# Segment loop of a recurrent-memory transformer: P V's middle tile for both heads in one matmul, weight slices asked for at their buffer's release, three loads on SyncE's queue

## The chip, the cores and the metric

The kernel runs on one core of a Trainium2 chip. The metric is device microseconds of one execution; lower is better. Engines are named as in the profile: PE (TensorE matmuls), PEld (its weight loads), DVE (VectorE), ACT (ScalarE), POOL (GpSimd), SP (SyncE, which here only issues DMAs).

## The reference

Everything is bfloat16. x is 2048 x 640.

```python
# part a: 64 segments of 32 rows, in order; mem (8 x 640) goes from one to the next
for s in range(64):
    h = concat([mem, x[32*s:32*s+32]])                   # 40 x 640
    q, k, v = h @ Wq, h @ Wk, h @ Wv                     # 32 heads of 192
    p = softmax(where(mask, q @ k.T * 192**-0.5, -1e9))  # per head, 40 x 40; mask: key < 8 or query >= key
    o = (p @ v).reshape(40, 32*192) @ Wo                 # 40 x 640
    mem, a[32*s:32*s+32] = o[:8], o[8:]
# part b: sliding attention with 8 keys at distance 2, 32 heads of 20
b = dilated_attention(x @ wqkv) @ wo
out = g * a + (1 - g) * b                                # g = sigmoid(sum(x * gate_w))
```

Each segment needs the memory of the segment before, so the 64 steps of part a are a chain.

## The kernel before

The work runs in four stages. From 0 to about 181 us part b and the gate are computed and stored. From 181 to 359 us a prepass projects, for all segments at once, 8 rows of each segment that do not depend on the memory (the "z" rows: their q, k and v go to zpk_dram). From 359.0 to 1652.4 us the segment loop runs (part_a). From there to the end, part_z projects the z rows' attention output through Wo.

In the loop a segment has 32 rows left that depend on the memory. Four heads' columns are put side by side on TensorE: its 128 columns hold four blocks of 32 rows, one for each j in 0 to 3, and every matmul is given a tile position 32j. Nearly all weights stay in SBUF. Fourteen slices of 384 KB (the list STREAM) do not fit: each segment loads them again from a scratch tensor in DRAM (wscr) into five buffers (WBUFS, pool wstream, tile wst). get_unit (L565 to L570) asks for a slice where the program first uses it; the load goes out on SP's queue as soon as the last matmul that read its buffer is done.

The order of PE, ACT and DVE is the order in which the program issues (manual_schedule); SP's order is the scheduler's, as early as the waits allow. One segment, by its lines:

- project (L771): q and k projections, six PSUM tiles (u = 0 to 2 for each); ACT copies each out (c_qk, L784); PE transposes them (t_qk, L792) and DVE copies the result (c_t, L803 and L807).
- s_a, s_b (L825, L834): scores of two halves of the heads, h = 0 and 1; e_exp (L843, ACT), e_mask (L847, DVE), e_norm (L857, PE, sums over the keys), e_recip_a (L862 and L863, ACT, reciprocals), e_recip_b (L869 and L870, DVE, the normalized P).
- m_v (L771): v projections u = 0, 1, 2; c_v copies them out (L881, DVE). V of the z rows (Vz) comes from zpk_dram by a load on ACT's queue (load_vz, L756).
- pv_half(h) (L883 to L906): P V. The 384 columns of two heads are three tiles of 128: t = 0 is the first head's, t = 2 the second's, and t = 1, the middle one, is half of either head. So t = 0 and t = 2 are full-tile matmuls (128 columns of V), t = 1 is made with two 64-column matmuls, each with its own head's P. The r < 2 matmuls (L897) use V of the 32 rows, the third (L902) Vz. A half is 48 matmuls. Its output lies in four PSUM banks: pS (two banks of psS) for j = 0 and 2, and two one-bank tiles px of the pool psx (two buffers) for j = 1 and 3. Below, J0 to J3 are the four outputs.
- c_x (L911) copies the 32 rows of each J out of PSUM, c_z (L918) the z rows' 8 columns into zst; both are shared between ACT ("a") and DVE ("d").
- o_group (L940): the out projection, in two PSUM accumulators, "oa" (384 columns of the output) and "ob" (256), twelve groups of four matmuls each. Groups 0 to 5 of a part use the result of pv_half(0), 6 to 11 that of pv_half(1).
- the copies of the accumulators to whi (L1030 and L1038, ACT), load_z for the next segment (L751, ACT's queue, and a POOL copy, L752), sel (L951, L954), which puts the new memory into the next segment's hT, and tail (L1046, L1050), which adds part b's rows (a4, loaded at L1000 on ACT's queue) and is followed by the store to out_dram (L1056, ACT's queue). hT of the next segment is loaded at L686 on ACT's queue. zst is stored to oz_dram at L1023 on ACT's queue.

Around the change the program's order is

```python
m_v(2, (0, 1, 2)); pos = pv_half(0); c_x(0, pos, (0, 1, 3), "add")
e_norm(1); e_recip_a(1); m_v(2, (3, 4)); c_v(2); e_recip_b(1)
c_x(0, pos, (2,), "a"); c_z(0, pos, (1, 3), "aa"); c_z(0, pos, (0, 2), "dd")
o_group("oa", 0 to 5); pos = pv_half(1); c_x(1, pos, range(4), "adda"); c_z(1, pos, range(4), "adad")
oz store; o_group("ob", 0 to 4); o_group("oa", 6 to 11); whi copy; load_z; o_group("ob", 5 to 11)
```

with the scores of the second half, s_a(2), s_a(3), s_b(1) and e_exp(1), ahead of it. At the loop's start five slices are loaded ahead, and w_ob's last weights (last_loads) are loaded during segment 0; in the last segment load_oz fetches the z rows' attention output into weight tiles that are no longer needed, and the first slice of "oa" goes into such a tile as well (L935).

## Time and profile before

| what | value |
|---|---|
| median of 3 runs | 1710.91 us (1705.75 to 1717.67) |
| the profiled execution | 1710.89 us |
| its span in the trace | 1709.1 us, mean PE clock 0.982 |
| segment loop | 359.0 to 1652.4 us |
| 62 steady segments | 382.8 to 1623.9 us |

In the groups of the profile a row reads: line, engine, operation, output<-input by the program's names, size; then busy us, mean ns of one; then idle time of the engine just before, with what released it. A row of the waits reads: engine, line <- what it waited for: us in total, times, longest. A row of the stretches has: start and end, length, then for PE, PEld, DVE, ACT, POOL busy us and (x instructions), then PE's granted clock, the DMA engines' busy share and GB/s. A row of the timeline reads: start, length, engine, line, operation, output<-input, size, how many; in brackets the idle time before it and what ended it. "issue" is time in which an engine waited for nothing that the profile shows. q1 is SP's DMA queue, q10 ACT's, q8 fetches instructions.

### The profile page before, as it was taken

Reading aid. Unit: us, or ns where it says so; the run is one execution under the profiler, and the core shown is the slowest. Engines: PE = TensorE matmul, PEld = TensorE weight load, DVE = VectorE, ACT = ScalarE, POOL = GpSimd, SP = SyncE. Lnnn points to the kernel's source line nnn. Section 1 sums busy time; section 2 is a strip of 40 time slices with the busy share of each in tenths; the row PEclk is TensorE's granted clock in tenths of the full one; section 3 lists DMA queues with packets and bytes.
Section 4 is the critical chain, followed back from the end, with each engine's and each line's share of the span. In section 5 each row is a group of like instructions: output and inputs, shape, how many; then the busy total and the mean of one; then the engine's idle time right before and its main releaser. Section 6 shows DMA issues by size and latency. Waiting matters only on the chain.

```text
span 1709.1 us, 75634 instructions
## 1 busy us (share of the span) xinstructions
PE 1602.0 (94%) x33193; PEld 888.6 (52%) x33209; DVE 697.0 (41%) x2159; ACT 803.7 (47%) x2082; POOL 60.0 (4%) x124
## 2 busy tenths in 40 slices
PE   7887999989999999999999999999999999999989
PEld 4544544445555555555555555555555545555559
DVE  3765333234444443444444443444443334444430
ACT  3877423234455444444454444445444444544450
POOL 2030000000000000000000000000000000000000
PEclk9998899999999999999999999999999999999999
DMA  7798798989999998999999999999999989999981
GB/s 200 188 221 203 217 326 222 262 248 311 310 309 313 306 299 294 307 305 303 308 312 294 300 312 301 298 303 309 306 312 303 296 290 304 310 301 306 301 278 31
DMA packets 307607, 479.43 MB, mean 281 GB/s; under 512 B 100556, under 2 KB 186444, under 8 KB 307276
## 3 DMA queue, kind: packets, MB, share of 16 engines
q1 hardware_dynamic: 208144, 418.12, 75.3%
q10 hardware_dynamic: 99132, 56.46, 11.8%
q8 instruction: 260, 4.26, 1.0%
q14 instruction: 71, 0.58, 0.1%
HBM read 432.76 MB, written 47.23 MB: 281 GB/s over the span
## 4 chain that ended last, share of the span: by engine, by line
PE 81%; DMA 11%; ACT 3%; issue 3%; DVE 1%; SPq 1%; ACTq 0%; DVEq 0%
PE ps_qk L771 25%; PE ps_wo L940 13%; PE ps_v L771 10%; PE ps_pre L622 6%; DMA TZ<-zpk_dram 5%; PE ps_qkT L792 5%; PE ps_S L825 4%; PE ps_oT L897 3%; PE ps_z L1104 3%; PE ps_pre L652 3%; DMA wst<-wscr 2%; ACT ZB L1030 2%; PE ps_bqk L236 1%; PE ps_S L857 1%; PE ps_mem L951 1%
## 5 line engine op out<-in xcount | busy, mean ns | idle before, releaser
L771 PEld LDWEIGHTS <-hT 128*32 128x32 bf16 x11520 | 275.3, 96 | 284.5 <-issue 15.3
L784 ACT CAST TZ<-ps_qk 128x512 bf16<-128x512 f32 x384 | 218.4, 586 | 318.6 <-PE ps_qk L771 318.6
L771 PE MATMUL ps_qk<-w_q,hT 128*32 128x512 bf16 x3264 | 267.7, 383 | 2.8 <-issue 2.8
L771 PE MATMUL ps_qk<-w_k,hT 128*32 128x512 bf16 x3264 | 265.5, 380 | 0.7 <-DVE ZV L81 0.4
L771 PE MATMUL ps_v<-w_v,hT 128*32 128x512 bf16 x3072 | 243.7, 383 | 0.0
L803 DVE COPY ZB<-ps_qkT 128x512 bf16<-128x512 bf16 (+1 forms) x256 | 91.0, 356 | 350.2 <-PE ps_qkT L792 254.0
L940 PEld LDWEIGHTS <-TZ 128*32 128x32 bf16 x6144 | 145.7, 96 | 105.8 <-ACT TZ L911 41.6
L940 PE MATMUL ps_wo<-w_oa,TZ 128*32 128x384 bf16 x2560 | 148.2, 330 | 10.4 <-issue 9.8
L881 DVE CAST TZ<-ps_v 128x512 bf16<-128x512 f32 (+1 forms) x256 | 137.0, 556 | 43.8 <-PE ps_v L771 43.7
L771 PE MATMUL ps_qk<-wst,hT 128*32 128x512 bf16 x1152 | 149.1, 381 | 0.5 <-DMA wst<-wscr 0.4
L911 ACT CAST TZ<-ps_oT 128x192 bf16<-128x192 f32 x256 | 75.8, 322 | 146.8 <-PE ps_oT L902 84.8
L911 DVE CAST TZ<-ps_oT 128x192 bf16<-128x192 f32 x256 | 85.7, 355 | 73.0 <-PE ps_oT L902 71.0
L940 PE MATMUL ps_wo<-w_ob,TZ 128*32 128x256 bf16 x2304 | 107.2, 274 | 8.8 <-issue 8.7
L954 DVE CAST hT<-ps_mem 128x24 bf16<-128x24 f32 x126 | 22.5, 179 | 220.7 <-PE ps_mem L951 220.7
L771 PE MATMUL ps_v<-wst,hT 128*32 128x512 bf16 x768 | 100.1, 385 | 8.9 <-DMA wst<-wscr 8.9
L792 PE MATMUL ps_qkT<-ident,TZ 128*128 128x128 bf16 x1536 | 107.5, 219 | 0.1
L792 PEld LDWEIGHTS <-TZ 128*128 128x128 bf16 x1536 | 88.6, 98 | 27.2 <-issue 27.0
L940 PE MATMUL ps_wo<-wst,TZ 128*32 128x256 bf16 (+1 forms) x1280 | 96.3, 301 | 3.3 <-issue 2.7
L843 ACT ACTIVATE ZB<-ps_S 32x224 bf16<-32x224 f32 x256 | 89.0, 348 | 9.4 <-PE ps_S L834 0.7
L843 ACT ACTIVATE TZ<-ps_S 32x224 bf16<-32x224 f32 x256 | 89.0, 348 | 9.4
L752 POOL COPY TZ<-ZB 128x384 bf16<-128x384 bf16 x64 | 32.6, 510 | 1477.1 <-DMA ZB<-zpk_dram 684.4
L825 PE MATMUL ps_S<-ZB,TZ 64*128 64x160 bf16 (+1 forms) x768 | 82.6, 234 | 0.0
(135 smaller groups left out, 2014.6 us busy)
## 6 DMA issues: line engine op xcount, KB each, us to landing
wst<-wscr SPq DMA_DIRECT2D x896, 384.0 KB
zpk_dram<-ZS ACTq DMA_DIRECT2D x4, 3072.0 KB
ZB<-zpk_dram ACTq DMA_DIRECT2D x64, 192.0 KB
zpk_dram<-ZV ACTq DMA_DIRECT2D x32, 192.0 KB
TZ<-zpk_dram ACTq DMA_DIRECT2D x64, 96.0 KB
oz_dram<-TZ ACTq DMA_DIRECT2D x64, 96.0 KB
w_q<-in_A_Wq_dram SPq DMA_DIRECT2D x14, 384.0 KB
w_k<-in_A_Wk_dram SPq DMA_DIRECT2D x14, 384.0 KB
```

Of the source, the lines that this page charges most:

```text
L622: nc.tensor.matmul(ps[:], lhsT=weights(j, kc, 6 * Rp + 3 * r + t), rhs=zTi[:, kc, :], start=(kc == 0), stop=(kc == KC - 1))
L652: mm = nc.tensor.matmul(pss[g][:], lhsT=zTi[:, kc, 128 * st:128 * st + 128], rhs=weights(kc, g), start=(kc == 0), stop=(kc == KC - 1))
L771: nc.tensor.matmul(ps[32 * j:32 * j + 32, :], lhsT=hT[:, kc, :], rhs=rhs, start=(kc == 0), stop=(kc == KC - 1), tile_position=(0, 32 * j), ...
L784: nc.scalar.copy(sts[i], pqs[i][:])
L792: nc.tensor.transpose(pT[:, 128 * t:128 * t + 128], st[:, 128 * t:128 * t + 128], self.ident[:])
L803: nc.vector.tensor_copy(QTf[:, run[2]:run[2] + 4, run[3]:run[3] + n, :].rearrange("p b x i -> p x b i"), src.rearrange("p (x b i) -> p x b ...
L825: nc.tensor.matmul(grid(h, par)[:, :, 0:80].rearrange("p j (b r i) -> p j b r i", r=2, i=8)[:, :, :, r, :], lhsT=KTs[3 * R + t][k0:k1, :], ...
L843: nc.scalar.activation(E[ps], pSs[h][ps, :, 112 * j:112 * j + 112], ACT.Exp, scale=scale_a)
L881: nc.vector.tensor_copy(VU[u][:, f0:f1], pvs[u][:, f0:f1])
L897: nc.tensor.matmul(out[:, r, t, :], lhsT=V[2 * h + r][ks, f0:f1], rhs=E[ks, par, 0:80].rearrange("p (b r i) -> p b r i", r=2, i=8)[:, :, r ...
L911: cp(oTxs[2 * h + j // 2][:, 6 * (j % 2):6 * (j % 2) + 6, :], pos[j][:, 0:240].rearrange("p (c q) -> p c q", q=40)[:, :, 8:40])
L940: nc.tensor.matmul(pso[part][32 * jj:32 * jj + 32, 0:n], lhsT=oTxs[2 * (g // 2) + J // 2][:, 6 * (J % 2) + 3 * (g % 2) + t, :], rhs=osl[pa ...
```

## The change

- pv_half: the middle tile is one matmul with 128 columns of V for both heads' P (80 columns of P, 32 for Vz). The upper half of the partitions then holds the second head's result in other columns. A half is 40 matmuls. px is one tile of two banks, and psx has one buffer (of two banks) instead of two (of one).
- the copies: c_pv makes a copy of one or two J (n) over all 128 partitions, and then a second, smaller one over partitions 64 to 127 that overwrites a part of the first with the second head's columns. Twenty copies a segment instead of sixteen, otherwise divided between ACT and DVE. c_v(2) goes from DVE to ACT.
- t_qk: tiles 0 to 3 share one two-bank psx tile, 4 and 5 use a tile of psm.
- load_next: a slice is asked for in the program right after the last matmul of the slice that had its buffer, in a fixed rotation. The load into a weight tile at L935 is gone.
- queues: V of z, hT and the last rows (a4) are loaded on SP's queue instead of ACT's; V of z is asked for ahead of e_exp(0) instead of behind it. The store of zst stays on ACT's queue, behind the whi copy and load_z (but for the last segment).

```diff
@@ -562,12 +562,16 @@
-    def get_unit(self, key):
-        if key in self.ahead:
-            return self.ahead.pop(key)
+    def load_next(self):
+        n = self.loaded
+        if n >= len(STREAM) * (self.S // self.seg):
+            return
+        self.loaded = n + 1
+        key = STREAM[n % len(STREAM)]
         t = self.wstream.tile([128, 1536], BF, name="wst", tag="wst")
         self.nc.sync.dma_start(t[:], self.wscr[key])
-        return t
+        self.ahead[key] = t
@@ -676,14 +680,14 @@
                 vts += [load_v(*v) for v in vs[len(vts):]]
-        for k in STREAM[:WBUFS]:
-            self.ahead[k] = self.get_unit(k)
+        self.loaded = 0
+        for _ in range(WBUFS):
+            self.load_next()
         hT = self.hTp.tile([128, self.KC, 32], BF, name="hT")
-        eng = self.nc.sync if s == 0 else self.nc.scalar
-        eng.dma_start(hT[:].rearrange("p c t -> p (c t)"), self.xh_dram[s])
+        self.nc.sync.dma_start(hT[:].rearrange("p c t -> p (c t)"), self.xh_dram[s])
         return hT
@@ -744,7 +748,7 @@
             psm = ctx.enter_context(tc.tile_pool(name="psm", bufs=2, space=bass.MemoryType.PSUM, reuse_waits="tile"))
-            psx = ctx.enter_context(tc.tile_pool(name="psx", bufs=2, space=bass.MemoryType.PSUM, reuse_waits="tile"))
+            psx = ctx.enter_context(tc.tile_pool(name="psx", bufs=1, space=bass.MemoryType.PSUM, reuse_waits="tile"))
             psS = ctx.enter_context(tc.tile_pool(name="psS", bufs=2, space=bass.MemoryType.PSUM, reuse_waits="tile"))
@@ -753,7 +757,7 @@
             def load_vz(s):
-                nc.scalar.dma_start(Vz, self.zpk_dram[s, :, 0:384])
+                nc.sync.dma_start(Vz, self.zpk_dram[s, :, 0:384])
@@ -765,11 +769,13 @@
                     for kc in kcs:
-                        st = self.get_unit((m, u, kc)) if (m, u, kc) in STREAM else None
+                        st = self.ahead.pop((m, u, kc)) if (m, u, kc) in STREAM else None
                         for j in range(4):
                                              stop=(kc == KC - 1), tile_position=(0, 32 * j), skip_group_check=True)
+                        if st is not None:
+                            self.load_next()
@@ -785,9 +791,11 @@
                     st = sts.pop(i)
-                    if i % 2 == 0:
-                        pTs["two"] = psx.tile([128, 2, 512], BF, tag="x", name="ps_qkT")
-                    pT = pTs["two"][:, i % 2]
+                    if i == 0:
+                        pTs["x"] = psx.tile([128, 4, 512], BF, tag="x", name="ps_qkT")
+                    elif i == 4:
+                        pTs["m"] = psm.tile([128, 2, 512], BF, tag="m", name="ps_qkT")
+                    pT = pTs["x"][:, i] if i < 4 else pTs["m"][:, i - 4]
                     for t in range(4):
@@ -877,45 +885,45 @@
                 def c_v(u):
+                    cp = nc.scalar.copy if u == 2 else nc.vector.tensor_copy
                     for f0, f1 in ((0, 256), (256, 512)) if u == 1 else ((0, 512),):
-                        nc.vector.tensor_copy(VU[u][:, f0:f1], pvs[u][:, f0:f1])
+                        cp(VU[u][:, f0:f1], pvs[u][:, f0:f1])
                     pS = psS.tile([128, 2, 512], F32, tag="S", name="ps_oT")
-                    px = [psx.tile([128, 512], F32, tag="x", name="ps_oT") for _ in range(2)]
-                    pos = [pS[:, 0], px[0], pS[:, 1], px[1]]
-                    po = [pos[j][:, 0:240].rearrange("p (r t q) -> p r t q", r=2, t=3) for j in range(4)]
-                    full, half = ((0, 0, 0, 128), (2, 1, 256, 384)), ((1, 0, 128, 192), (1, 1, 192, 256))
-                    for r, chunks in ((0, full), (1, full), (2, full), (0, half), (1, half), (2, half)):
-                        for t, par, f0, f1 in chunks:
-                            p0 = 64 if f0 == 192 else 0
+                    px = psx.tile([128, 2, 512], F32, tag="x", name="ps_oT")
+                    for t, f0, f1 in ((0, 0, 128), (2, 256, 384), (1, 128, 256)):
+                        for r in range(4 if t == 1 else 3):
                             for j in range(4):
-                                ks = slice(32 * j, 32 * j + 32)
-                                out = po[j][p0:p0 + f1 - f0]
-                                if r < 2:
-                                    nc.tensor.matmul(out[:, r, t, :], lhsT=V[2 * h + r][ks, f0:f1],
-                                                     rhs=E[ks, par, 0:80].rearrange("p (b r i) -> p b r i", r=2, i=8)[:, :, r, :],
-                                                     start=(r == 0 and t == 0),
-                                                     stop=False, tile_position=(32 * j, p0), skip_group_check=True)
+                                ks, o = slice(32 * j, 32 * j + 32), (pS, px)[j % 2][:, j // 2, 40 * t + 120 * (r % 2):512]
+                                Q = (E[ks, :, 0:80] if r < 2 else E[ks, :, 80:112]).rearrange(
+                                    "p a (b r i) -> p a b r i", r=2, i=8)
+                                if t == 1:
+                                    rhs, out = Q[:, :, :, r % 2, :], _ap(o, [[200, 2], [1, 40 if r < 2 else 16]])
+                                elif r < 2:
+                                    rhs, out = Q[:, t // 2, :, r, :], o[:, 0:40]
                                 else:
-                                    nc.tensor.matmul(out[:, :, t, 0:16], lhsT=Vz[ks, f0:f1],
-                                                     rhs=E[ks, par, 80:112].rearrange("p (b r i) -> p r b i", r=2, i=8),
-                                                     start=False, stop=(t == 1), tile_position=(32 * j, p0),
-                                                     skip_group_check=True)
-                    return pos
-                def c_x(h, pos, js, engs):
-                    for j, eng in zip(js, engs):
-                        cp = nc.scalar.copy if eng == "a" else nc.vector.tensor_copy
-                        cp(oTxs[2 * h + j // 2][:, 6 * (j % 2):6 * (j % 2) + 6, :],
-                           pos[j][:, 0:240].rearrange("p (c q) -> p c q", q=40)[:, :, 8:40])
-                def c_z(h, pos, js, engs):
-                    for j, eng in zip(js, engs):
-                        c0 = 24 * h + 6 * j
-                        cp = nc.scalar.copy if eng == "a" else nc.vector.tensor_copy
-                        cp(oTz[:, c0:c0 + 6, :], pos[j][:, 0:240].rearrange("p (c q) -> p c q", q=40)[:, :, 0:8])
+                                    rhs, out = Q[:, t // 2].rearrange("p b r i -> p r b i"), _ap(o, [[120, 2], [1, 16]])
+                                nc.tensor.matmul(out, lhsT=(V[2 * h + r] if r < 2 else Vz)[ks, f0:f1], rhs=rhs,
+                                                 start=(r == 0 and t == 0), stop=(r == 3), tile_position=(32 * j, 0),
+                                                 skip_group_check=True)
+                    return pS, px
+                def c_pv(dst, pos, j, n, eng, q0, nq):
+                    cp = nc.scalar.copy if eng == "a" else nc.vector.tensor_copy
+                    x, c = slice(j // 2, j // 2 + n), 6 * (j % 2)
+                    p = pos[j % 2]
+                    cp(dst[:, x, c:c + 6, :], p[:, x, 0:240].rearrange("p x (c q) -> p x c q", q=40)[:, :, :, q0:q0 + nq])
+                    cp(dst[64:128, x, c + 1:c + 5:3, :],
+                       p[64:128, x, 240:480].rearrange("p x (r w) -> p x r w", r=2)[:, :, :, q0:q0 + nq])
+                def c_x(h, pos, j, n, eng):
+                    c_pv(self.TZ[:, 768 * h:768 * h + 768].rearrange("p (x c q) -> p x c q", x=2, q=32), pos, j, n, eng, 8, 32)
+                def c_z(h, pos, j, n, eng):
+                    c_pv(zst[:, 192 * h:192 * h + 192].rearrange("p (x c q) -> p x c q", x=2, q=8), pos, j, n, eng, 0, 8)
@@ -931,17 +939,15 @@
                         if (part, i) not in osl:
-                            if s + 1 == nseg and sum(k[0] in ("oa", "ob") for k in STREAM) > WBUFS and i2 == 0 and part == "oa":
-                                w = self.res_tiles[self.oz_free.pop()]
-                                nc.sync.dma_start(w[:], self.wscr[part, i])
-                            else:
-                                w = self.get_unit((part, i))
+                            w = self.ahead.pop((part, i))
                             osl[part, i] = w[:].rearrange("p (c f) -> p c f", c=4 if part == "oa" else 6)
                                          tile_position=(0, 32 * jj), skip_group_check=True)
+                        if (part, i) in STREAM and all(self.wo_place(part, b)[0] != i for b in order[4 * i2 + jj + 1:]):
+                            self.load_next()
@@ -980,8 +986,8 @@
                 s_a(0, FULL); s_a(1, FULL); s_b(0, FULL)
+                load_vz(s)
                 e_exp(0)
-                load_vz(s)
                 t_qk(4); t_qk(5)
@@ -997,7 +1003,7 @@
                     self.load_oz(0)
-                nc.scalar.dma_start(a4[:], self.bsc_dram[32 * s:32 * s + 32, :].rearrange("t (j f) -> j t f", j=4))
+                nc.sync.dma_start(a4[:], self.bsc_dram[32 * s:32 * s + 32, :].rearrange("t (j f) -> j t f", j=4))
                 m_v(1, (0,))
@@ -1007,20 +1013,19 @@
                 pos = pv_half(0)
-                c_x(0, pos, (0, 1, 3), "add")
+                c_x(0, pos, 0, 1, "a"); c_x(0, pos, 1, 2, "d"); c_x(0, pos, 2, 1, "d")
                 e_norm(1)
                 e_recip_b(1)
-                c_x(0, pos, (2,), "a")
-                c_z(0, pos, (1, 3), "aa")
-                c_z(0, pos, (0, 2), "dd")
+                c_z(0, pos, 0, 2, "a"); c_z(0, pos, 1, 2, "d")
                 for i2 in range(6):
                 pos = pv_half(1)
-                c_x(1, pos, range(4), "adda")
-                c_z(1, pos, range(4), "adad")
-                nc.scalar.dma_start(self.oz_dram[s], zst)
+                c_x(1, pos, 0, 1, "a"); c_x(1, pos, 1, 2, "d"); c_x(1, pos, 2, 1, "a")
+                c_z(1, pos, 0, 2, "a"); c_z(1, pos, 1, 2, "d")
+                if s + 1 == nseg:
+                    nc.scalar.dma_start(self.oz_dram[s], zst)
                 if s + 1 == nseg:
@@ -1030,6 +1035,7 @@
                     load_z(s + 1)
+                    nc.scalar.dma_start(self.oz_dram[s], zst)
                     pm = psS.tile([128, 2, 512], F32, tag="S", name="ps_mem")
@@ -1041,7 +1047,7 @@
                 def tail(s=s):
-                    pa = psx.tile([128, 512], F32, tag="x", name="ps_a")
+                    pa = psx.tile([128, 2, 512], F32, tag="x", name="ps_a")[:, 0]
                     for jj in range(4):
```

## The prediction

> **What bounds the kernel now.** First the page: busy shares, the DMA row, the chain that ended last.
>
> ```profile
> PE 1602.0 (94%) x33193; PEld 888.6 (52%) x33209; DVE 697.0 (41%) x2159; ACT 803.7 (47%) x2082; POOL 60.0 (4%) x124
> ...
> PE 81%; DMA 11%; ACT 3%; issue 3%; DVE 1%; SPq 1%; ACTq 0%; DVEq 0%
> ```
>
> TensorE is the bound. What is not TensorE's in the chain is DMA (11%) and "issue" (3%, 51 us). Then the stretches: first segment, 62 steady segments, last segment.
>
> ```profile
> 359.00:382.80 23.80, 18.32 (x404) 10.16 (x407) 8.14 (x27) 8.79 (x27) 0.00 (x0) 0.93 0.89 273
> 382.80:1623.90 1241.10, 1189.34 (x27598) 649.92 (x27594) 515.36 (x1798) 601.61 (x1736) 31.59 (x62) 1.00 0.92 304
> 1623.90:1652.40 28.50, 22.66 (x477) 11.79 (x466) 10.31 (x34) 13.05 (x32) 0.51 (x1) 0.88 1.01 330
> ```
>
> A steady segment takes 1241.1/62 = 20.02 us with PE busy 96% of it at full clock and DMA engines busy 92%. A quiet one takes 19.38 (from one L1030 copy at 1260.41 to the next at 1279.79). The first and last take 23.8 and 28.5. The waits inside the steady stretch say where the 0.64 between 20.02 and 19.38 goes:
>
> ```profile
> PE ps_wo L940 <- issue: 20.5, 23, 1.8
> ...
> PEld L902 <- DMA TZ<-zpk_dram: 13.5, 16, 1.6
> ```
>
> With PE's smaller "issue" rows (3.2, 3.1, 1.3) that is 28.1 us, 0.45 a segment; late V of z costs 13.5, 0.22 a segment. In the trace every "issue" stall of that kind begins at a PE instruction whose running number has the same remainder by 256, and 2.2 to 2.7 us after a 16 KB packet of the instruction queue (q8: 260 packets, 4.26 MB) starts: they are instruction fetches, late where PE works through many short instructions. Nearly all fall in the out-projection just behind the second P V half, every second segment. Last, the timeline around the change, in the quiet segment:
>
> ```profile
> 1275.17 0.27 PE L897 MATMUL ps_oT<-TZ 32*128 32x40 bf16 x16
> ...
> 1275.83 0.62 DVE L911 CAST TZ<-ps_oT 128x192 bf16<-128x192 f32 x2 [0.26 <-PE ps_oT L902]
> ...
> 1276.41 1.08 PE L940 MATMUL ps_wo<-w_oa,TZ 128*32 128x384 bf16 x20
> ...
> 1277.23 0.21 DVE L870 TENSOR_TENSOR ZB<-ZB,ps_S 128x64 bf16<-128x64 bf16 x1
> 1277.37 0.32 DVE L918 CAST TZ<-ps_oT 128x48 bf16<-128x48 f32 x2
> 1277.50 0.17 PEld L897 LDWEIGHTS <-TZ 32*128 32x128 bf16 x16 [0.40 <-DVE ZB L870]
> 1277.51 0.28 PE L897 MATMUL ps_oT<-ZB,TZ 32*128 32x40 bf16 x16
> ...
> 1278.58 0.51 PE L940 MATMUL ps_wo<-w_oa,TZ 128*32 128x384 bf16 x8
> ```
>
> pv_half(1) starts 2.34 us after pv_half(0), released by the normalization L870, while PE is just done with its oa groups (24 matmuls from 1276.24 end at 1277.49). The z copies (L918) run beside it. So DVE has no slack here: what is put ahead of pv_half(1) on DVE shows at once.
>
> **The change, part by part.** Sizes below are for one segment; the profiled execution is 1710.89 us (span 1709.1 and 1.8 around it), the median of the runs 1710.91, so the sum stands against both.
>
> *(a) P V.* A half's 24 full-tile matmuls start within 0.15 us, then come a gap of 0.10 where the tile shape changes and 24 half-tile starts in 0.11. Instead: 24, then 16 of twice the columns, no change of shape. An estimate from these starts: 0.15 + 0.12 instead of 0.36, so 0.09 less a half.
>
> *(b) The copies.* 16 become 20, since every copy of P V gets a second one ("fix") over partitions 64 to 127 that overwrites part of the first and waits for it. And px is now one buffer: pv_half(1) can't start before c_z(0) is done, which on DVE stands behind L870. Durations of n elements from the rows by shape: DVE 199, 355, 692 ns at 48, 192, 512, so about 0.148 + 0.00106n; ACT 212, 322, 586, so 0.172 + 0.00081n; an independent DVE copy starts 0.07 + 0.00104n after the one before (1275.831 to 1276.106 at 192), a dependent one 0.03 after its end. From pv_half(0)'s first matmul: copies start at 0.665 − 0.09 = 0.575. J1 and J3 in one copy (384): to 1.13; fix (128) 1.16 to 1.45; J2 (192) 1.37 to 1.72; fix (64) 1.75 to 1.97; L869 1.89 to 2.20; L870 to 2.33; c_z (96) 2.26 to 2.51; fix (32) 2.54 to 2.72; 0.05 to PE: 2.78 instead of 2.34, so +0.44. ACT's chain (J0, its fix, two reciprocals of 0.29, c_v(2) 0.59, c_z and fix) comes to about 2.55 and does not decide. The oa groups end at about 2.37, so PE stands still 0.4 us where it did not.
>
> *(c) Behind pv_half(1)* the next oa group needs ACT's J0 copy and fix: 0.61 + 0.33 + 0.03 + 0.22 + 0.05 = 1.24 after pv_half(1) instead of 1.07: +0.17. So (a) to (c) give +0.61 a segment, 64 times: +39 us. If the fixes overlap the copy ahead more than supposed, DVE's chain is 0.25 shorter (+23 in all); if each fix costs 0.05 more, +52.
>
> *(d) V of z on SP's queue.* It is asked for one step earlier in program order and on SP, about 0.25 us sooner. On ACT's queue it takes 3.8 us (median) from issue to last packet and PE could start 4.5 after issue; a slice of four times its size takes 3.5 on SP's. So it would be just in time, or still late sometimes: −8 of the 13.5 (0 to −13.5; the loss side is a rival). [...]
>
> *(e) Instruction fetch.* Per half 8 matmuls and their 8 weight loads go: 32 PE instructions fewer. Between a fetch's trigger and the end of its 256 instructions now lie 0.4 + 0.2 us of new waiting and fewer instructions, so a stall of 0.89 (20.5/23) shrinks to about 0.3. Of 28 us I take −18, with 0 (the wait lies ahead of the trigger) and −28 as ends. Two segments hold 1792 = 7 × 256 PE instructions now, so the stall keeps its place; 864 instead of 896 a segment lets it wander, which could as well raise it by 5 elsewhere.
>
> *(f) The loop's ends.* In the first segment PE waits 5.44 us for a slice (374.09), behind w_ob's loads on SP; asked for at its buffer's release it leads them: −4. In the last, 3.46 (1641.13), behind the loads of load_oz, which now come later: −3.5. Inside the loop the request changes nothing: SP's own waits for the slices are on PE releases already (302.0 on L940, 281.8 and 210.1 on L771), so it goes out at the release in both. Ends 0 and −9.
>
> *(g) At nothing:* c_v(2) on ACT (ACT has the 0.2 shown in (b); without it pv_half(1) moves one for one); t_qk(4,5) in psm, where m_v(1) must await c_t(5) (that copy ends 1271.95, m_v(1) starts 1272.17: 0.2 spare); the later oz store (lands 4.1 after its issue, some 1.5 before c_qk(3) needs its place); three issues (0.33, 0.60, 0.55) off ACT, whose exponentials kept their 0.36 step beside them; SP takes them beside 14 slices' 0.32 each. POOL's copy still follows load_z alone. The load of the last rows waits on SP for the out store's landing, 4.25 after its issue, long past by then in a quiet segment; queued behind it are two slices and the next V of z. Ends 0 and +25.
>
> Sum: 39 − 8 − 18 − 7.5 = +5.5; 1710.9 + 5.5 ≈ 1716.
>
> **The rivals.** *One, slower: the fetch gives nothing back.* If the fetch is triggered only after the new wait, PE's stalls stay and the copies' +39 stands with half of (d): 39 − 4 − 7.5 = +28, 1739. It decides when PE's "issue" rows stay above 20 us. For it: the L940 stalls begin after pv_half(1), while part of the new wait is before. Against: the new 0.2 of (c) is just there. [...]
> *Two, slower: V of z waits in SP's order*, behind slices or the last rows' wait. A slice's 384 KB at 304 GB/s is 1.26 us; less the 0.25 and the 0.67 between 3.8 and 4.5 leaves PE 0.35 a segment, 22 us, and (d)'s 8 are not won: 1716 + 30 ≈ 1747. It decides when V of z lands over 4.8 us after the time of its issue now. SP's waits, all on PE, speak against.
> *Three, faster: copies cheap, stalls gone.* DVE's chain 0.25 shorter (+23), all of (d), 24 of (e), 9 of (f): 23 − 13.5 − 24 − 9 = −23.5, 1687. For it: PE's quiet segment shows no other loss. Against: every fix waits for its copy.
> *Four: the early request is no request at the ends either* ((f) is 0): 1724, inside the first forecast's range.
>
> **How the numbers follow.** Forecast with four: 0.43, itself 1700 to 1728; one 0.25; two 0.12; three 0.20. 1% is 17 us, about what a measurement can tell from no change: below 1694 faster 0.20, above 1728 slower 0.37, between 0.43. The range reaches to three and two and leaves a tenth out at each side: 1686 to 1745.
>
> **What would show it.** (b): PE's first matmul of pv_half(1) released by DVE's c_z fix instead of L870, 2.7 to 2.85 after pv_half(0), PE idle 0.3 to 0.5. (c): oa again 1.2 to 1.3 after pv_half(1). (d): the P V wait on zpk_dram under 7 us. (e): PE "issue" near 10 us. (f): first segment under 20.5, last under 25.5. I am wrong if DVE's chain ends before the oa groups, if SP stands waiting for the out store, or if V of z's wait grows.

## The result, and the profile after

The changed kernel takes 1760.6 us (median of 4 runs, 1756.14 to 1764.13), the kernel before 1708.3 in the same comparison: ratio 1.0298, 95% interval 1.0245 to 1.0351. It is 52 us slower, and outside the range that was forecast (1686 to 1745). The profiled execution took 1762.1 us, its span is 1760.4.

The page of the changed kernel: TensorE is as busy as before (94%), but less of the chain that ended last is TensorE's, and DMA and DVE have more of it.

```profile
PE 1646.9 (94%) x32169; PEld 896.4 (51%) x32185; DVE 739.5 (42%) x2223; ACT 893.3 (51%) x2274; POOL 59.8 (3%) x124
...
PE 62%; DMA 21%; DVE 8%; ACT 4%; issue 3%; SPq 2%; ACTq 0%; DVEq 0%
```

The DMA share of the chain went from 11% to 21%, DVE's from 1% to 8%. PE's instructions fell by 1024 matmuls (16 in each of 64 segments) as they should.

The stretches of the changed kernel, cut at the ends of its first and its 63rd segment:

```profile
359.00:382.80 23.80, 18.86 (x384) 10.55 (x372) 8.23 (x27) 10.63 (x30) 0.00 (x0) 0.86 0.91 288
382.80:1676.00 1293.20, 1236.58 (x26582) 665.01 (x26586) 556.50 (x1860) 687.76 (x1922) 31.44 (x62) 0.99 0.89 291
1676.00:1703.50 27.50, 23.30 (x510) 12.70 (x501) 10.89 (x34) 16.11 (x36) 0.51 (x1) 1.00 1.00 325
```

The steady stretch grew from 1241.1 to 1293.2 us, so all of the 52 us is there. Between whi copies (L1030 before, L1035 after) a steady segment takes 20.87 us on average instead of 20.02. The quietest twentieth takes 20.09 instead of 19.05: +1.04 is there in every segment. What the mean has above that, the stalls, fell from 0.97 to 0.78.

The waits of PE in the steady stretch of the changed kernel (total, times, longest):

```profile
PEld L908 <- DMA TZ<-zpk_dram: 29.7, 39, 3.4
...
PEld L908 <- DVE TZ L919: 22.9, 62, 0.6
...
PE ps_wo L944 <- issue: 6.8, 9, 2.0
```

Late V of z went from 13.5 to 29.7 us. A new wait stands at pv_half(1), on DVE's second z copy (L919), in all 62 segments. Instruction fetch, by the idle rows, went from 28.1 to 6.8. And the queue of SP has a wait that the kernel before did not have there:

```profile
SPq L1006 <- DMA out_dram<-ZB: 110.2, 61, 2.6
```

L1006 is the load of the last rows: in 61 segments SP stands still for 1.8 us on average until the out store has landed.

The timeline of one segment of the changed kernel, from the copies behind pv_half(0) to the oa groups behind pv_half(1):

```profile
1254.94 0.56 DVE L918 CAST TZ<-ps_oT 128x384 bf16<-128x384 f32 x1 [0.80 <-PE ps_oT L908]
...
1255.53 0.29 DVE L919 CAST TZ<-ps_oT 64x128 bf16<-64x128 f32 x1
...
1255.86 0.36 DVE L918 CAST TZ<-ps_oT 128x192 bf16<-128x192 f32 x1
...
1256.25 0.23 DVE L919 CAST TZ<-ps_oT 64x64 bf16<-64x64 f32 x1
1256.51 0.32 DVE L877 TENSOR_TENSOR ZB<-ZB,ps_S 128x160 bf16<-128x160 bf16 x1
...
1256.96 0.09 PEld L908 LDWEIGHTS <-TZ 32*128 32x128 bf16 x1 [0.32 <-DVE ZB L878]
...
1257.16 0.20 DVE L919 CAST TZ<-ps_oT 64x32 bf16<-64x32 f32 x1
1257.41 0.36 PEld L908 LDWEIGHTS <-TZ 32*128 32x128 bf16 x39 [0.36 <-DVE TZ L919]
...
1258.64 0.29 DVE L919 CAST TZ<-ps_oT 64x128 bf16<-64x128 f32 x1
...
1258.99 0.28 PEld L944 LDWEIGHTS <-TZ 128*32 128x32 bf16 x12 [0.24 <-DVE TZ L919]
...
1260.02 0.48 ACT L1035 CAST ZB<-ps_wo 128x384 bf16<-128x384 f32 x1 [0.46 <-PE ps_wo L944]
```

From the first DVE copy to the px matmuls of pv_half(1) are 1257.41 − 1254.94 = 2.47 us; before it was 1277.51 − 1275.83 = 1.68. One matmul goes ahead (1256.96, the weight load of J0, which needs no px); the next one writes px and waits. Both new waits of PE end with an L919, a second copy. And every DVE instruction behind an L919 starts only after that copy's end, 31 or 32 ns after it where it waits for nothing else.

### The profile page after: what moved, and what is told of

It reads as the page before. It is cut to its first block, busy times and chain, and to the rows that moved or that the text cites. A ratio compares the mean times of both kernels' runs of the same rounds, so it can differ in the third digit from the quotient of the medians.

```text
span 1760.4 us, 73765 instructions
## 1 busy us (share of the span) xinstructions
PE 1646.9 (94%) x32169; PEld 896.4 (51%) x32185; DVE 739.5 (42%) x2223; ACT 893.3 (51%) x2274; POOL 59.8 (3%) x124
## 4 chain that ended last, share of the span: by engine, by line
PE 62%; DMA 21%; DVE 8%; ACT 4%; issue 3%; SPq 2%; ACTq 0%; DVEq 0%
PE ps_qk L775 24%; DMA TZ<-zpk_dram 11%; PE ps_wo L944 10%; PE ps_qkT L800 4%; PE ps_v L775 4%; DVE TZ L918 4%; PE ps_oT L908 3%; PE ps_S L833 3%; PE ps_pre L626 3%; PE ps_pre L656 3%; PE ps_z L1110 2%; DVE TZ L919 2%; ACT ZB L1035 2%; PE ps_mem L957 1%; DMA zpk_dram<-ZS 1%
## 5 line engine op out<-in xcount | busy, mean ns | idle before, releaser
L775 PEld LDWEIGHTS <-hT 128*32 128x32 bf16 x11520 | 275.2, 96 | 274.6 <-DVE hT L960 13.7
L944 PEld LDWEIGHTS <-TZ 128*32 128x32 bf16 x6144 | 162.0, 96 | 123.1 <-DVE TZ L919 38.6
L944 PE MATMUL ps_wo<-w_oa,TZ 128*32 128x384 bf16 x2560 | 201.2, 336 | 5.2 <-issue 4.9
L918 DVE CAST TZ<-ps_oT 128x384 bf16<-128x384 f32 (+2 forms) x320 | 126.9, 396 | 102.0 <-PE ps_oT L908 98.0
L918 ACT CAST TZ<-ps_oT 128x192 bf16<-128x192 f32 (+1 forms) x320 | 92.0, 288 | 143.9 <-PE ps_oT L908 140.7
L944 PE MATMUL ps_wo<-wst,TZ 128*32 128x256 bf16 (+1 forms) x1280 | 117.6, 305 | 2.2 <-issue 1.4
L944 PE MATMUL ps_wo<-w_ob,TZ 128*32 128x256 bf16 x2304 | 112.3, 275 | 0.6 <-issue 0.5
L890 DVE CAST TZ<-ps_v 128x256 bf16<-128x256 f32 (+1 forms) x192 | 92.6, 510 | 39.8 <-PE ps_v L775 39.7
L908 PEld LDWEIGHTS <-TZ 32*128 32x128 bf16 x5120 | 54.5, 92 | 104.8 <-DMA TZ<-zpk_dram 35.2
```

Of the source, the lines that this page charges most:

```text
L775: nc.tensor.matmul(ps[32 * j:32 * j + 32, :], lhsT=hT[:, kc, :], rhs=rhs, start=(kc == 0), stop=(kc == KC - 1), tile_position=(0, 32 * j), ...
L890: cp(VU[u][:, f0:f1], pvs[u][:, f0:f1])
L908: nc.tensor.matmul(out, lhsT=(V[2 * h + r] if r < 2 else Vz)[ks, f0:f1], rhs=rhs, start=(r == 0 and t == 0), stop=(r == 3), tile_position= ...
L918: cp(dst[:, x, c:c + 6, :], p[:, x, 0:240].rearrange("p x (c q) -> p x c q", q=40)[:, :, :, q0:q0 + nq])
L944: nc.tensor.matmul(pso[part][32 * jj:32 * jj + 32, 0:n], lhsT=oTxs[2 * (g // 2) + J // 2][:, 6 * (J % 2) + 3 * (g % 2) + t, :], rhs=osl[pa ...
```

## The experiments

Times are medians; each ratio is against runs of the kernel before on the same chip, with its 95% interval. "Quiet" is the lowest twentieth of the segments, "stall" the mean less that.

### The change taken apart

The P V change alone, on the kernel before (pv_half, copies, c_v(2) on ACT, t_qk's tiles, psx):

```diff
-pos = pv_half(0); c_x(0, pos, (0, 1, 3), "add")
+pos = pv_half(0); c_x(0, pos, 0, 1, "a"); c_x(0, pos, 1, 2, "d"); c_x(0, pos, 2, 1, "d")
...
-c_z(0, pos, (1, 3), "aa"); c_z(0, pos, (0, 2), "dd")
+c_z(0, pos, 0, 2, "a"); c_z(0, pos, 1, 2, "d")
```

> The kernel before with only the P V change: 40 instead of 48 matmuls a half, px as one buffer, copies with a second one over partitions 64 to 127, c_v(2) on ACT, t_qk's tiles. Queues and requests as before. Theory 1: pv_half(1)'s px matmuls start about 3.04 us after pv_half(0) in a quiet segment (2.34 before) and the stretch from there to the whi copy is 2.6 (2.28 before), so +1.0 a segment in quiet ones, less some 0.3 of instruction-fetch stalls: +0.6 a segment, about 1745. Theory 2, the queue did it: about 1715. Issue waits of PE at L940's successor near 10 us instead of 20.5 if the new wait covers the fetches.

Measured: 1726.1 us, ratio 1.0117 (1.0065 to 1.0168). The quiet segment is 20.09, so the whole +1.04 is P V's; but the stalls fall from 0.97 to 0.20, so only +17 us of it reach the time. Both theories missed the size: the stalls gave back 0.76 and not 0.3. In PE's rows both kinds of stall shrink, the fetch from 20.5 and late V of z, still on ACT's queue here, from 13.5:

```profile
PEld L902 <- DMA TZ<-zpk_dram: 5.9, 14, 2.0
...
PE ps_wo L942 <- issue: 3.5, 6, 1.5
```

The request alone (load_next in place of get_unit, and the load at L935 gone):

```diff
-st = self.get_unit((m, u, kc)) if (m, u, kc) in STREAM else None
+st = self.ahead.pop((m, u, kc)) if (m, u, kc) in STREAM else None
...
+if st is not None:
+    self.load_next()
```

> The kernel before with only the slices asked for right behind the last matmul of the buffer's slice (load_next), and no load into a resident tile in the last segment. Theory: inside the loop SP waits for PE's releases in both, so steady segments stay at 20.0 us; only the loop's ends can change, the last segment from 28.5 to about 25 and the first not (it was 23.8 in both kernels): about 1704 to 1708. Rival: the request's place reorders SP against the other loads and the mean segment changes by more than 0.1 us: more than 6 us either way.

Measured: 1705.4, ratio 0.9984 (0.9956 to 1.0012): no difference that the runs can tell. The last segment went from 27.9 to 25.4 us as expected, the steady ones stayed (20.07).

The three loads on SP's queue alone, with the later store of zst:

```diff
-nc.scalar.dma_start(Vz, ...)  # and hT, and a4
+nc.sync.dma_start(Vz, ...)
```

> The kernel before with only the three loads on SP's queue (V of z ahead of e_exp(0)) and the later store of zst. Theory 1: the last rows' load stands on SP's queue until the out store has landed, the slices behind it go out bunched and V of z behind those: SP waits near 100 us on out_dram, V of z lands 0.3 to 0.5 us later in the segment, the P V wait on zpk_dram grows to 25 to 30 us, about 1722 to 1726. Rival: the queue alone is harmless because PE reaches pv_half(0) at the same time and only the P V change makes it early enough to wait: about 1708, wait on zpk_dram near 13.

Measured: 1803.3, ratio 1.0588 (1.0531 to 1.0645): +94 us, more than five times what was expected. The direction was right, the mechanism had a larger price here: the waits of SP in this kernel (up to 1640 us, 59 of the 62 segments) are

```profile
SPq L569 <- PE ps_wo L939: 209.2, 173, 3.5
SPq L999 <- DMA out_dram<-ZB: 146.0, 59, 3.5
```

and PE waits 55.7 us for V of z and 17.7 for slices in the same stretch. The same three loads taken back from the changed kernel:

```diff
-nc.sync.dma_start(Vz, ...)  # and hT, and a4; V of z behind e_exp(0) again
+nc.scalar.dma_start(Vz, ...)
```

> The changed kernel with V of z, hT and the last rows on ACT's queue again, V of z behind e_exp(0) as before; P V, copies and load_next as changed. Theory 1, copies and queue: of the +52 us about +17 come from V of z (P V's waits on zpk_dram 29.7 us changed, 13.5 before), the rest from the copies around pv_half(1), which this kernel keeps: about 1743 us, the PEld wait on zpk_dram 10 to 16 us. Theory 2, copies alone: V of z is late for the same reasons on either queue; about 1760, the wait stays near 30. Theory 3, the queue is most of it: about 1725.

Measured: 1730.3, ratio 1.0142 (1.0095 to 1.0189), wait on zpk_dram 11.6. The queue moves cost 30 of the 52 us, the P V change most of the rest: between theories 1 and 3.

### Which of the three loads

Only the last rows back on ACT's queue in the changed kernel:

```diff
-nc.sync.dma_start(a4[:], self.bsc_dram[...])
+nc.scalar.dma_start(a4[:], self.bsc_dram[...])
```

> The changed kernel with only the load of the last rows on ACT's queue again; V of z and hT stay on SP's. So far: all three loads back on ACT's queue gave 1730 us instead of 1760, so the queue is worth 30. Theory 1, SP stands still: the last rows' load waits on SP until the out store has landed (110 us in 61 segments), and two slices and V of z behind it go out late and bunched. Then this kernel alone gets most of the 30 back: 1733 to 1742, SP waits on out_dram gone, V of z landing 14.0 us after the whi copy instead of 14.6, P V's wait on zpk_dram 10 to 16 us instead of 29.7. Theory 2, V of z's place in the slices' row is the loss whatever is ahead of it: 1755 to 1762, first packet still 2.3 us after the issue, wait near 25.

Measured: 1723.9, ratio 1.0086 (1.0059 to 1.0114), so this one line is 37 us. PE's waits for V of z, which is still on SP's queue:

```profile
PEld L908 <- DMA TZ<-zpk_dram: 1.9, 4, 0.8
...
PE ps_oT L908 <- DMA TZ<-zpk_dram: 1.4, 3, 0.7
```

29.7 became 1.9. Theory 1 holds, by more than it forecast (1733 at best, a wait of 10), and theory 2 falls. The issue times after the whi copy (medians in us, read from the trace) show how:

| SP's DMA | changed | last rows on ACT |
|---|---|---|
| slice | 6.38 | 6.38 |
| last rows | 8.74 | (ACT) |
| slice | 9.38 | 8.14 |
| slice | 9.89 | 9.22 |
| V of z | 10.43 | 9.87 |

The out store is issued 3.87 after the whi copy, and the load of the last rows gets out 4.85 after that, at 8.72. The slice behind it was free to go at 8.14. So two slices and V of z leave SP bunched and late; V of z lands 14.6 after the whi copy instead of 13.7. One segment of the changed kernel, whose whi copy starts at 779.15 (the rows' load 8.74 after it):

```profile
787.89 0.53 SPq L1006 DMA_DIRECT2D ZB<-bsc_dram  x1
788.53 0.90 SPq L573 DMA_DIRECT2D wst<-wscr  x2
789.53 0.37 SPq L760 DMA_DIRECT2D TZ<-zpk_dram  x1
```

And one with the last rows on ACT's queue, whi copy at 761.72:

```profile
768.10 3.16 SPq L573 DMA_DIRECT2D wst<-wscr  x3
771.58 0.32 SPq L760 DMA_DIRECT2D TZ<-zpk_dram  x1
```

V of z alone back on ACT's queue, behind e_exp(0):

```diff
-nc.sync.dma_start(Vz, self.zpk_dram[s, :, 0:384])
+nc.scalar.dma_start(Vz, self.zpk_dram[s, :, 0:384])
```

> The changed kernel with only V of z on ACT's queue again, behind e_exp(0); hT and the last rows stay on SP's. Theory 1, SP stands still at the last rows' load: V of z then escapes that (lands near 13.9 after the whi copy, P V's wait on it 10 to 15 us), but two slices a segment still go out late, so some of the loss stays where slices come late: 1742 to 1750, and waits of PE on slices appear or stay. Theory 2, V of z behind the slices is the whole loss: 1730 to 1735, like all three loads moved back.

Measured: 1738.8, ratio 1.0170 (1.0122 to 1.0218), between the two theories. SP still waits 115.8 us for the out store. PE's wait on zpk_dram is 13.8 us and not 1.9, on slices only 3.0: on its own queue V of z escapes SP's order, but with the slices still going out bunched on SP's it lands 14.2 after the whi copy, against 13.7 with the last rows moved. So the loss that stays is V of z again, less than theory 1 had it, and not the slices that it named.

The last rows alone on SP's queue, in the kernel before:

```diff
-nc.scalar.dma_start(a4[:], self.bsc_dram[...])
+nc.sync.dma_start(a4[:], self.bsc_dram[...])
```

> The kernel before with only the load of the last rows on SP's queue. So far: all three loads and the later zst store on the kernel before gave 1803 instead of 1709, +94, with SP waiting 146 us on out_dram and three slices right behind. Theory 1: this one load is the larger part, since it stands at the head of SP's queue until the out store lands: +40 to +90 (1750 to 1800), waits of PE on slices (17.7 us there) and of SP on out_dram above 100. Theory 2: V of z or hT on SP is what costs: within 15 of 1709.

Measured: 1795.8, ratio 1.0507 (1.0455 to 1.0558): +87 of the 94 us. Its waits of PE, and of SP (up to 1640 us, 59 of the 62 segments):

```profile
PE ps_v L771 <- DMA wst<-wscr: 41.7, 41, 1.8
...
PEld L902 <- DMA TZ<-zpk_dram: 20.3, 19, 2.5
```

```profile
SPq L1000 <- DMA out_dram<-ZB: 155.9, 59, 3.6
```

Here the load stands one slice further ahead in SP's order: the slice that went out at 6.38 goes out at 9.37, three slices bunch, and V of z, asked for on ACT's own queue at the same 10.08, still lands 0.8 later (14.93 instead of 14.14). In the changed kernel only two slices are held up by the load, and the same line costs 37. That this is the reason for the smaller price is argued: the two kernels differ in P V as well.

### The copies

The second copies over all partitions, from partition 0 (they then overwrite the lower half's values as well):

```diff
-cp(dst[64:128, x, c + 1:c + 5:3, :], p[64:128, x, 240:480]...)
+cp(dst[:, x, c + 1:c + 5:3, :], p[:, x, 240:480]...)
```

> The changed kernel with the second copies over all 128 partitions instead of 64 to 127, same columns, so the lower half's values are wrong. In the changed kernel an instruction behind such a copy starts 24 to 31 ns after its end, behind full copies 83 to 104 ns before it. Theory 1: that is because it covers part of the partitions; then the next instruction here overlaps again, DVE's chain from the first copy to c_z's end is shorter by 2 x 0.115 us, the px matmuls of pv_half(1) start about 2.8 instead of 3.04 us after pv_half(0) in a quiet segment, and the time falls by 14 to 22 us, to 1738 to 1746. Theory 2: it is because the second copy waited for its own engine, so the next starts after its end here too: 1760, chain unchanged.

Measured: 1743.3, ratio 1.0183 (1.0126 to 1.0239). DVE's copies in this kernel:

```profile
1266.97 0.56 DVE L918 CAST TZ<-ps_oT 128x384 bf16<-128x384 f32 x1 [1.45 <-PE ps_oT L908]
...
1267.56 0.29 DVE L919 CAST TZ<-ps_oT 128x128 bf16<-128x128 f32 x1
...
1267.77 0.35 DVE L918 CAST TZ<-ps_oT 128x192 bf16<-128x192 f32 x1
...
1268.15 0.23 DVE L919 CAST TZ<-ps_oT 128x64 bf16<-128x64 f32 x1
1268.29 0.31 DVE L877 TENSOR_TENSOR ZB<-ZB,ps_S 128x160 bf16<-128x160 bf16 x1
```

The copy at 1267.77 starts before the end of the one at 1267.56 again, and L877 starts 1.32 us after the first copy instead of 1.57. The copies last as long as on 64 partitions (0.29 and 0.23 us). Theory 2 falls, and 17 us hang on which partitions the second copies work on. The edit changes two things at once, how many partitions (64 or 128) and where they begin (64 or 0), so that theory 1's reason, covering a part, is not shown. Other instructions in the traces speak against it: in part b of the kernel before, ACT's instructions over 63 partitions from partition 0 (L276 and L79) let the next one start 95 to 111 ns before their end in the five cases where it did not wait for something else. The loop's exponentials, four over 32 partitions that begin at 0, 32, 64 and 96, each start 12 ns (11 to 13) after the end of the one before. So both were measured on fewer than 128 partitions, a start before the end and one after it, and the number alone does not tell them apart; what does is not shown. A copy over 64 partitions from partition 0 would tell; none was run.

The z copies of px on ACT, ahead of the reciprocals, with the last rows on ACT's queue:

```diff
+c_z(0, pos, 1, 2, "a")
 e_norm(1); e_recip_a(1); m_v(2, (3, 4)); c_v(2); e_recip_b(1)
-c_z(0, pos, 0, 2, "a"); c_z(0, pos, 1, 2, "d")
+c_z(0, pos, 0, 2, "d")
```

> The changed kernel with the load of the last rows on ACT's queue (that alone gave 1723.9 us) and with the z copies of px moved from DVE, behind L878, to ACT, ahead of the reciprocals; those of pS go to DVE. Theory: pv_half(1) waits for the z copies out of its single px buffer; on ACT they end early, so L878 releases it again. ACT's reciprocals come 0.45 us later, which moves L877 and L878 by 0.1 to 0.2, so the px matmuls start about 2.75 instead of 3.04 us after pv_half(0) in a quiet segment: 12 to 18 us less, 1706 to 1712. Rival: the reciprocals' delay on ACT eats it all, or the px buffer is not what holds: 1720 to 1728.

Measured: 1737.2, ratio 1.0152 (1.0115 to 1.0188), 13 us slower than without the swap, and above the rival's range too. The rival's mechanism holds, at a higher price:

```profile
1257.69 0.24 ACT L918 CAST TZ<-ps_oT 128x96 bf16<-128x96 f32 x1 [0.45 <-PE ps_wo L944]
...
1257.96 0.18 ACT L919 CAST TZ<-ps_oT 64x32 bf16<-64x32 f32 x1
...
1258.17 0.29 ACT L870 ACTIVATE ps_S<-ps_S 128x160 f32<-128x160 f32 x1
...
1258.81 0.32 DVE L877 TENSOR_TENSOR ZB<-ZB,ps_S 128x160 bf16<-128x160 bf16 x1 [0.56 <-ACT ps_S L871]
```

ACT's z copy had to wait 0.45 itself, the reciprocals came that much later again, and L877 now waits for them. pv_half(1) is held by whichever of the two chains is last; shortening one by lengthening the other lost time.

### Instruction fetch

The kernel before without the 16 matmuls that add V of z to the middle tile (that part of the output is left out):

```diff
-for r, chunks in ((0, full), (1, full), (2, full), (0, half), (1, half), (2, half)):
+for r, chunks in ((0, full), (1, full), (2, full), (0, half), (1, half)):
```

> The kernel before without the 16 matmuls a segment that add V of z to the middle tile, so the output lacks that part; nothing else is changed. PE has then 864 instead of 896 instructions a segment, as the changed kernel, but no new wait. It tells why PE's instruction-fetch stalls fell with the P V change (the issue rows of PE matmuls in the steady segments: 28.1 us before, about 8 with the P V change alone). Theory 1, the new waits ahead of and behind pv_half(1) cover the fetches: here they stay, 15 to 28 us, spread over more places since the boundary wanders by 32 instructions a segment. Theory 2, the count alone does it, because 896 x 2 = 7 x 256 held one boundary in the dense stretch: under 12 us, and the time falls by 10 to 20 to 1690 to 1700.

Measured: 1680.8, ratio 0.9822 (0.9792 to 0.9853). PE's fetch waits in the 62 steady segments fell from 28.1 to 13.5, between the two theories, with no new wait (the rows shown go on to 1640 us, past the 62 segments):

```profile
PE ps_wo L940 <- issue: 9.1, 19, 1.0
...
PE ps_oT L897 <- issue: 3.6, 6, 1.1
...
PE ps_qk L771 <- issue: 1.6, 3, 0.8
```

The time fell by more than these 15 us. The idle rows leave out what the modelled end of a matmul covers. Counted from start to start at every 256th PE instruction, against the same instruction's median over the segments, the fetch stalls are 43 us in the kernel before and 24 here. These 19 us, 2.6 less of late V of z and 4 of the quiet segment (0.07 shorter) are nearly all of the 27 us by which the steady stretch is shorter.

To try the place of the boundary between two fetches alone: small matmuls once in the first segment, 32, 64 or 96 PE instructions, on the kernel before with the harmless parts of the change (below).

```diff
+for _ in range(16):  # 32, 48
+    nc.tensor.matmul(pd[:, 0:8], lhsT=self.ident[:], rhs=self.ident[:, 0:8], start=True, stop=True, ...)
```

> The kernel before with load_next and V of z and hT on SP's queue (1704.0 us), and with 16 small extra matmuls (32 PE instructions with their weight loads, some 1 to 2 us) once, in the first segment. Inside the loop nothing changes but where each 256th PE instruction falls: 32 instructions earlier in every segment, and it stays there, since two segments hold 7 x 256. Theory 1, the place of the boundary sets the fetch stalls (28 to 33 us of PE issue in steady segments): with the place the stalls change, and over the three shifts of 32, 64 and 96 they differ by more than 10 us among each other and from 1704, some below 1690. Theory 2, the stalls come with the dense stretch wherever the boundary falls: all three within 5 of 1705.

> As the kernel with 32 extra PE instructions, with 64 (32 small matmuls, some 2 to 4 us once). Theory 1: the boundary is now half-way between its two places of before; PE's issue waits in steady segments change by over 10 us and the time with them, to 1680 to 1692 if it leaves the dense stretch behind pv_half(1). Theory 2: 1704 to 1709.

> As the kernel with 32 extra PE instructions, with 96 (48 small matmuls, some 3 to 5 us once). Theory 1: PE's issue waits in steady segments differ from those at 32 and 64 by several us, and the time follows them. Theory 2: 1705 to 1710.

Measured: 1709.7, 1704.4, 1711.4, ratios 0.9998 (0.9965 to 1.0031), 0.9974 (0.9940 to 1.0009), 1.0012 (0.9976 to 1.0047). The largest row of the fetch waits is 27.6, 23.2 and 26.5 us (24.6 without the shift), in each case at the out projection:

```profile
PE ps_wo L942 <- issue: 27.6, 27, 2.5
```

Neither 10 us among the three nor a time below 1690 came (and 1711.4 is outside theory 2's 5 us as well), but that does not decide against theory 1, because the shift changes less than was thought. A segment has 892 PE instructions in the trace (890 matmuls and weight loads and two of the sequencer), not 896, and 1784 is 7 × 256 less 8. So in these kernels the boundary moves by 8 instructions every two segments and passes nearly all places within the 62, padded or not. Within one trace the place does show: of the 217 packets in the steady segments of the kernel before, 40 are followed by an idle row of over 0.15 us, and 34 of these rows are at P V or at the out projection.

### What is left of the change when its costs are taken out

The kernel before with load_next, V of z and hT on SP's queue and the later store of zst; the last rows on ACT's queue, P V as before:

```diff
-nc.scalar.dma_start(Vz, self.zpk_dram[s, :, 0:384])
+nc.sync.dma_start(Vz, self.zpk_dram[s, :, 0:384])
 nc.scalar.dma_start(a4[:], self.bsc_dram[...])
```

> The kernel before with the parts that did not cost: slices asked for by load_next, V of z (ahead of e_exp(0)) and hT on SP's queue, zst stored later; the last rows stay on ACT's queue and P V is the old one. Theory: nothing on SP waits for the out store, V of z lands near 13.7 us after the whi copy instead of 14.1, P V's wait on zpk_dram falls from 13.5 to 2 to 5 us, the fetch stalls (28 us) stay: 1694 to 1700. Rival: V of z on SP only works with the P V change, which starts segments later; then 1705 like the request alone.

Measured: 1704.0, ratio 0.9962 (0.9941 to 0.9983): the same as before within 2%, with an interval just below 1. The three padded kernels, which differ from it by those few matmuls alone, do not bear out a gain (0.9974 to 1.0012). The wait on zpk_dram fell from 13.5 to 9.1, and to 3.8, 6.3 and 3.5 in the padded ones, so this row differs by several us from trace to trace; the time is some 4 us above the range of the theory.

## Why the prediction was wrong

The forecast was 1716, +5.5 us; the step that failed is one that was costed at nothing in (g), the load of the last rows on SP: "long past by then in a quiet segment". It was not. What was needed stood in the trace of before: the store is issued 3.87 us after the whi copy, its last packet ends 4.2 us later and its last semaphore update comes 4.7 us later, at about 8.5 (in the changed kernel that update comes 4.8 after the issue, and the load that waits for the store gets out at 4.85), while the slices that SP's new order puts behind this load are due at 8.14 and 9.22. In the changed kernel the load got out at 8.7. That is 37 us of the 52 (the kernel with this one line taken back), with an end given as +25. I held the landing against the moment at which the rows were asked for before, 10.9, and not against the moment that SP's order now gave it. Two of the prediction's own signs of being wrong came: SP stood waiting for the out store, and V of z's wait grew.

With that line taken back the kernel takes 1724, inside the range. That this lies so near is partly luck, because two errors of the sum then cancel in part: its quiet segments cost 65 us and not 39, and its stalls fall by 49 and not by the 26 of (d) and (e).

Two readings of the trace of before were off. The quiet segment of 19.38 us holds a fetch stall near its start:

```profile
1261.64 0.10 PEld L940 LDWEIGHTS <-TZ 128*32 128x32 bf16 x2 [0.32 <-issue]
```

The quietest segments take 19.05, so 0.97 us a segment were stalls and not 0.64, and there was more to give back than the 28.1 and 13.5 of the idle rows. And a segment has 892 PE instructions and not 896, so the boundary between two fetches did not keep its place before the change either.

Point by point:

- (a) Right. The copies start 0.575 us after pv_half(0) in quiet segments, as worked out.
- (b) The direction and the releaser were right (the px matmuls wait for DVE's z copy), the size not: +0.44 forecast, 2.47 − 1.68 − 0.09 = +0.70 measured. The first matmul did start at 2.75, near the 2.78 of the forecast, but released by L878 and alone. The chain was built on copies that start before the one ahead ends; behind a second copy, over partitions 64 to 127, they start 31 ns after its end (the kernel with full second copies gave 0.25 us back, 1.57 to 1.32).
- (c) +0.17 forecast, +0.33 measured (px matmuls to whi copy 1260.02 − 1257.41 = 2.61 instead of 2.28). PE resumes as forecast, then waits again for J1 (1258.99 in the timeline), whose copy is now one of 384 with J3's and has a second one behind it. The forecast had no such second wait. Together (a) to (c) are +1.04 a quiet segment instead of +0.61: 65 us instead of 39 before anything is given back.
- (d) Right in direction for V of z by itself: with the last rows on ACT's queue its waits are 1.9 with V of z and hT on SP's queue, 11.6 with these two on ACT's. How much of this is the queue's is less sure, since P V alone, with V of z on ACT's, had 5.9. In the changed kernel they are 29.7, because of (g). This is the second rival's mechanism, by its second half ("the last rows' wait"); its first half, a place behind slices, was not what cost. With the last rows off SP, V of z took 3.7 us from issue to last packet on SP's queue, on ACT's in the kernel before 3.8, so the move by itself shows no loss here.
- (e) −18 forecast, 28.1 to 6.8 measured by the idle rows, −21: right in size by that measure. Counted from start to start it is 43 to 11, −32. As for its two parts, fewer instructions alone give about half (13.5 by the idle rows), and the new waiting by difference the rest; the waiting alone was not run. The first rival, by which nothing is given back, falls.
- (f) −7.5 forecast, about −1.4 measured: the last segment gained 3.0 (27.91 to 24.92), the first only 0.5 instead of 4, and the tail behind the loop lost 2.1 (57.18 to 59.24). In the first segment the slice's wait of 5.44 us went as forecast, but one for V of z came in its place:

```profile
PE ps_oT L908 <- DMA TZ<-zpk_dram: 4.6, 1, 4.6
```

The first segment's end varied from 376 to 384 us over the runs.

In sum: quiet segments +65, stalls −12 (fetch −32, late V of z +16, other stalls +4), ends −1.4, which is the +51 of the two spans.

## What to carry to other kernels

Before a load with a wait is moved to another engine's queue, write down when that wait ends and when each entry behind it would have gone; here the whole of SP's queue stood for the difference, 110 us in 61 segments, and with the last rows' load alone moved three slices left bunched on SP's queue and V of z, asked for at the same time on ACT's, landed 0.8 us later than in the kernel before. A copy that must repair part of another can cost more than its own length: here, on DVE, it started 34 or 35 ns after the end of the first, and the next instruction 31 or 32 ns after its own end. And stalls that are no part of the quiet case can shrink when a change makes the quiet case longer, so the price of a change is not the price in its quiet segment (+1.04) but what the stalls leave of it (+0.27 for P V alone).

## What the runs showed of the hardware

In the changed kernel, behind a copy over partitions 64 to 127, the next instruction of the engine, which works from partition 0, started 31 or 32 ns (DVE) or 23 to 26 ns (ACT) after that copy's end, in every case in which it waited for nothing else; in the kernel with full second copies, behind the same copy over all 128 partitions, 0.08 and 0.09 us (DVE) and 0.10 us (ACT) before its end. On ACT instructions over 63 partitions from partition 0 let the next one start 95 to 111 ns before their end, so there a number of partitions under 128 brought no such wait; what brings it is not shown, since no run changes the number or the beginning alone. Copies over 64 and over 128 partitions last the same (0.29 us for 128 elements, 0.23 for 64).

The instruction queue q8 moved 260 packets of 16 KB for 66402 instructions of PE and PEld, in the changed kernel 252 for 64354: about 255 to a packet. In the kernel before, 40 of the 217 packets of the steady segments were late by the idle rows, and PE went on 2.2 to 2.7 us after the start of such a packet. With 892 instructions a segment, the place of every 256th moved by 8 instructions every two segments. The stalls halved when 32 of 892 instructions a segment were left out (28.1 to 13.5 us by the idle rows, 43 to 24 from start to start); why they fell that much is not shown.

A load that waited on SP's queue for a store on ACT's held up what came behind it: the store's last packet ended 4.2 us after its issue, the load got out 4.85 us after it, and slices due at 8.14 and 9.22 went out at 9.38 and 9.89.
